# Two neighbouring blocks in one product for half of the off-diagonal products, and the Gram products ahead of `sp` and of half of `up`

## The chip, the cores and the metric

The kernel runs on one core of one Trainium2 chip. The metric is device time in microseconds (us) for one execution. The core has a matrix engine, TensorE (PE in the profile, its weight loads apart as PEld), and VectorE (DVE), ScalarE (ACT), GpSimd (POOL) and the queue of SyncE (SP), which issues transfers.

## What is computed

Three layers in a row. The first is an attention with a state that every token changes; its output is the input of two feed-forward layers.

```python
for t in range(S):                       # S = 768, 4 batches x 8 heads, D = 48
    kt, vt, bt = (k_n[:, :, t], v[:, :, t], beta[:, :, t, None])
    y[:, :, t] = np.einsum('bhd,bhde->bhe', q[:, :, t], state)
    v_old = np.einsum('bhde,bhd->bhe', state, kt)
    state = state + bt[:, :, :, None] * np.einsum('bhd,bhe->bhde', kt, vt - v_old)

a = x @ w_a                              # x: 3072 x 384, w_a, w_b: 384 x 1536
b = x @ w_b
x = a * b @ w_out
h = x @ w_in                             # 384 x 2048
g = np.maximum(h, 0.0) + alpha * np.minimum(h, 0.0)
out = g @ w_out2
```

## The kernel before

**Stages.** The 768 tokens are cut into six stages (`c` = 0 to 5) of 128 tokens, and a stage into two chunks (`j`) of 64. The 32 heads of all batches lie as 16 blocks times two halves of the partitions, called `x` (partitions 0 to 63 and 64 to 127). So a tile such as `ef`, `hw` or `TT` holds 32 blocks (16 for each `j`) of 64 tokens for each half.

**The chain of a stage.** For each stage the attention runs a chain of small products on TensorE, with copies and sums by ACT and DVE between them: `g` (Gram matrices of keys, and of keys with queries), the inversion of a 64 x 64 triangle for every block, `rp` (the part of the values that the state already holds), `up` (the triangle applied to the values), `sp` (the new state) and `yp` (the output). The inversion is done on the two 32 x 32 halves of the diagonal by DVE, and the 32 x 32 corner that is left comes from two products on TensorE, one after the other, both written to banks named `w`: first `w<-hw,ef` (the corner of `ef` times `hw`), whose eight copies go to the other half of `hw`, and then `w<-TT,hw`, whose eight copies go to `TT`. That is `offdiag`, for stages 1 to 5. Stage 0 has a function of its own, `first_sides`, with banks `w` and `xx`.

**How `w` is tiled.** In `offdiag` a product takes one block: 32 partitions deep (the low or the high 32 of a half), a stationary operand of 32 columns and a moving one of 32. There are 32 blocks and two halves, so 64 products for each of the two steps. The order is `i` (0 to 7), `q` (0 to 3), `x`, with block 8q + i at output partitions 32q. The two steps use one half each of the same two banks.

**The Gram products.** `mate` makes the products of a later stage's keys: eight products `g` of 64 x 128, in a bank of their own (`pre`, one buffer), dealt out among the products of another small step, which calls `beside(i)` after its `i`-th round. When the step is done, DVE takes the bank apart (`keep`: one copy to `ef`, two masked products to `Z`). In stages 2 to 4 `rp` and `up` are dealt by a pattern (`uneven`) in which `g` already stands first; `sp` always, and `up` in stage 1, run by the simple loop.

**The feed-forward work.** The first feed-forward layer is made of large products of 128 x 512 (`p`, `o<-g,wu`) that need the attention of a stage, and run beside the chain of the next one. The second layer (`h`, `o<-g,v`) follows from about 614 us on.

**What sets the order.** All instructions are first recorded, then put in order by a planner in the kernel (`Schedule`), which keeps a clock of its own for every engine and, at each step, takes the ready piece of work with the longest chain behind it. Successive small products are one piece (a block); large ones are single. So an edit of one small step may change the order on every engine. All recorded instructions carry line 203, and tiles are named by their names.

Of the kernel before, what the change touches and what calls it, by code (L numbers as in the profile page):

```python
# [5 lines left out]
F32 = mybir.dt.float32  # L6
# [550 lines left out]
class Attention:  # L557
# [80 lines left out]
    def norms(s, L, ef=None, late=False, sq=None):  # L638
# [4 lines left out]
        L["ef"] = ap.tile([128, 32, 64], F32, tag="ef", name="ef", bufs=1) if ef is None else ef  # L643
        sq = L["ef"][:, :, 0:48] if sq is None else sq
# [20 lines left out]
    def scale_values(s, L, j):  # L665
# [7 lines left out]
        s.spend(POOL, 7)  # L673

# [19 lines left out]
    def mate(s, L, j, i4, tag, then=None):  # L694

        def begun():
# [13 lines left out]
            def keep():  # L710
                nc.vector.tensor_scalar(L["ef"][:, j * 16 + i4 : j * 16 + i4 + 4, :], g[:, :, 0, :], -1.0, None, ALU.mult)
# [21 lines left out]
    def keep_keys(s, L, j, i8, g):  # L733

        s.nc.scalar.activation(L["ef"][:, j * 16 + i8 : j * 16 + i8 + 8, :], g, AF.Copy, scale=-1.0)
# [15 lines left out]
    def fold(s, L, j, other=None):  # L751

        e = L["ef"][:, j * 16 : j * 16 + 16, :]
        for sl, copy in ((slice(32, 64), s.nc.scalar.copy), (slice(96, 128), other or s.nc.scalar.copy)):
            copy(e[sl, :, 0:32], e[sl, :, 32:64])
            s.spend(ACT, 2.5)

    def inverting(s, L, room):
# [7 lines left out]
        nc.vector.transpose(a0, L["ef"][:, :, 0:32].rearrange("p a t -> p t a"))  # L766
# [11 lines left out]
    def inverting_halves(s, L, tag):  # L778
# [4 lines left out]
        nc.vector.transpose(eu, L["ef"][:, :, 0:32].rearrange("p a t -> p t a"))  # L783
# [51 lines left out]
    def offdiag(s, L):  # L835
# [4 lines left out]
        room = [s.bank("w").rearrange("p (n i t) -> p n i t", n=2, t=32) for _ in range(2)]  # L840
        for n, (here, left, right, there, to) in enumerate((
            (low, ef[:, :, 32:64], hw, high, hw),
            (high, hw, TT[:, :, 32:64], low, TT[:, :, 32:64]),
        )):
            banks = [t[:, n] for t in room]
            for i in range(8):
                for q in range(4):
                    for x in range(2):
                        nc.tensor.matmul(
                            banks[x][32 * q : 32 * q + 32, i, :],  # L850
                            left[here[x], 8 * q + i, :], right[here[x], 8 * q + i, :], start=True, stop=True,
                        )
            for q in range(4):
                for x in range(2):
                    nc.scalar.copy(to[there[x], 8 * q : 8 * q + 8, :], banks[x][32 * q : 32 * q + 32])
# [3 lines left out]
    def first_sides(s, L):  # L859
# [6 lines left out]
        for j in range(2):  # L866
# [3 lines left out]
            (low, ef[:, :, 32:64], hw, high, hw, [s.bank("w") for _ in range(2)]),  # L870
# [16 lines left out]
    def step(s, c, j, L, mates=(), joined=False, wide=False):  # L887
# [21 lines left out]
        def dealt(parts, beside):  # L909
# [11 lines left out]
            for i in range(8):  # L921
                for n, (o, _) in enumerate(parts):
                    yield n, i, o + i
                beside(i)
# [692 lines left out]
```

## Time and profile before

| | us |
|---|---|
| median of 3 runs | 1011.21 (1011.08 to 1015.61) |
| the profiled execution, own time | 1013.88 |
| its span | 1011.7 |
| PE busy | 991.9 (98%) |
| DVE, POOL, ACT busy | 612.4, 493.9, 461.4 |

A product of f32 leaves two records in the trace, so a block of 64 products is shown as x128. The ends of matrix products are modelled: a record's duration (some 0.19 us for a small one) is how long it takes to come through, and not how much room it takes; the room is read from the starts. A block's last start is its first start plus its length less one record's duration. The chain of work that ended last (part 4 of the page) tells whose time is the kernel's time. The order that the planner makes is shown below as rows of instructions in a row on one engine.

### The profile page before, as it was taken

Reading aid. Unit: us, or ns where it says so; the run is one execution under the profiler, and the core shown is the slowest. Engines: PE = TensorE matmul, PEld = TensorE weight load, DVE = VectorE, ACT = ScalarE, POOL = GpSimd, SP = SyncE. Lnnn points to the kernel's source line nnn. Section 1 sums busy time; section 2 is a strip of 40 time slices with the busy share of each in tenths; the row PEclk is TensorE's granted clock in tenths of the full one; section 3 lists DMA queues with packets and bytes.
Section 4 is the critical chain, followed back from the end, with each engine's and each line's share of the span. In section 5 each row is a group of like instructions: output and inputs, shape, how many; then the busy total and the mean of one; then the engine's idle time right before and its main releaser. Section 6 shows DMA issues by size and latency. Waiting matters only on the chain.

```text
span 1011.7 us, 23674 instructions
## 1 busy us (share of the span) xinstructions
PE 991.9 (98%) x10028; PEld 812.0 (80%) x10028; DVE 612.4 (61%) x1223; ACT 461.4 (46%) x845; POOL 493.9 (49%) x402
## 2 busy tenths in 40 slices
PE   7979999999999999999999999999999999999998
PEld 6767777888888788788878888888888888888886
DVE  7789867856795787567667677343343343433333
ACT  5936784474547355645588785122121221211211
POOL 4467854644664265546557986333333333333332
PEclk8899999999999999999999999999999999999999
DMA  9545423002301210000025542001020020000000
GB/s 216 194 144 181 148 70 94 32 2 66 95 1 33 62 68 1 18 19 31 19 80 174 170 136 84 1 25 38 1 63 1 1 63 0 32 1 1 32 1 32
DMA packets 27082, 61.40 MB, mean 61 GB/s; under 512 B 4320, under 2 KB 8928, under 8 KB 26976
## 3 DMA queue, kind: packets, MB, share of 16 engines
q1 hardware_dynamic: 26544, 59.50, 19.3%
q8 instruction: 78, 1.28, 0.5%
q10 hardware_dynamic: 432, 0.39, 0.1%
q14 instruction: 28, 0.23, 0.1%
HBM read 50.44 MB, written 9.44 MB: 59 GB/s over the span
## 4 chain that ended last, share of the span: by engine, by line
PE 90%; DMA 3%; POOL 2%; issue 2%; ACT 1%; DVE 1%; SPq 0%; DVEq 0%; POOLq 0%; ACTq 0%
PE o L203 33%; PE p L203 26%; PE h L203 19%; PE g L203 3%; PE yp L203 2%; PE spin L203 2%; PE up L203 2%; POOL W L203 1%; PE rp L203 1%; PE sp L203 1%; PE w L203 1%; DMA Z<-in_qt_dram 1%; POOL wu L203 1%; DMA b<-in_beta_dram 1%; DMA Z<-in_w_o_dram 1%
## 5 line engine op out<-in xcount | busy, mean ns | idle before, releaser
L203 PE MATMUL p<-x,wu 128*128 128x512 f32 x1296 | 318.5, 394 | 0.3 <-DVE x L203 0.3
L203 PEld LDWEIGHTS p<-x,wu 128*128 128x128 f32 x1296 | 240.8, 188 | 53.6 <-issue 2.6
L203 POOL TENSOR_TENSOR g<-neg,g 128x512 fp32r<-128x512 f32 x95 | 124.0, 1305 | 261.3 <-ACT g L203 257.8
L203 POOL TENSOR_TENSOR wu<-W,wu 128x384 fp32r<-128x384 f32 (+1 forms) x122 | 173.5, 1425 | 145.1 <-ACT wu L203 143.6
L203 PE MATMUL o<-g,v 128*128 128x512 f32 x870 | 211.5, 388 | 0.0
L203 PE MATMUL h<-x,v 128*128 128x512 f32 x864 | 211.3, 389 | 0.0
L203 DVE TENSOR_SCALAR neg<-h,al 128x512 f32<-128x512 f32 (+1 forms) x97 | 72.2, 744 | 228.8 <-PE h L203 228.7
L203 ACT CAST g<-neg 128x512 fp32r<-128x512 f32 (+1 forms) x97 | 59.8, 616 | 302.9 <-DVE neg L203 288.4
L203 PEld LDWEIGHTS o<-g,v 128*128 128x128 f32 x870 | 162.3, 188 | 33.7 <-ACT g L203 0.2
L203 PEld LDWEIGHTS h<-x,v 128*128 128x128 f32 x864 | 162.2, 188 | 33.7
L203 PE MATMUL o<-g,wu 128*128 128x512 f32 x648 | 164.9, 394 | 1.3 <-ACT g L203 1.1
L203 PEld LDWEIGHTS o<-g,wu 128*128 128x128 f32 x648 | 119.9, 188 | 28.2 <-ACT g L203 1.5
L203 ACT CAST wu<-W 128x768 fp32r<-128x768 f32 (+1 forms) x144 | 96.9, 676 | 80.8 <-PE p L203 59.0
L203 POOL TENSOR_TENSOR g<-a,g 128x512 fp32r<-128x512 f32 x57 | 78.7, 1380 | 40.6 <-ACT g L203 34.6
L203 DVE TENSOR_TENSOR inv<-inv,itmp 128x110 f32<-128x110 f32 (+12 forms) x256 | 75.0, 293 | 8.2
L203 ACT COPY a<-p 128x512 f32<-128x512 f32 x72 | 42.2, 586 | 64.9 <-PE p L203 43.8
L203 DVE SCALAR_TENSOR_TENSOR neg<-h,neg 128x512 f32<-128x512 f32 (+1 forms) x97 | 66.5, 686 | 3.3
L203 PE MATMUL g<-Z 48*64 48x64 f32 (+1 forms) x1024 | 62.8, 265 | 4.5 <-DMA Z<-in_kt_dram 1.9
L203 DVE TENSOR_TENSOR a<-p,a 128x512 f32<-128x512 f32 x59 | 40.5, 687 | 37.9 <-PE p L203 19.7
L203 PEld LDWEIGHTS g<-Z 48*64 48x64 f32 x1024 | 47.3, 148 | 12.4 <-issue 6.1
L203 DVE TENSOR_TENSOR itmp<-inv,gd 128x96 f32<-128x96 f32 (+8 forms) x150 | 40.6, 271 | 9.5 <-ACT gd L203 4.9
L203 ACT CAST g<-a 128x512 fp32r<-128x512 f32 x59 | 36.6, 620 | 6.0 <-DVE a L203 5.5
(110 smaller groups left out, 930.6 us busy)
## 6 DMA issues: line engine op xcount, KB each, us to landing
v<-in_w_o_dram SPq DMA_DIRECT2D x16, 384.0 KB, 3.5
v<-in_w_in_dram SPq DMA_DIRECT2D x16, 384.0 KB, 3.6
Z<-in_kt_dram SPq DMA_DIRECT2D x24, 192.0 KB, 3.6
Z<-in_qt_dram SPq DMA_DIRECT2D x24, 192.0 KB, 4.4
v<-in_vn_dram SPq DMA_DIRECT2D x12, 384.0 KB, 3.2
x2d<-x2s SPq DMA_DIRECT2D x18, 256.0 KB, 2.2
xf<-x2d SPq DMA_DIRECT2D x18, 256.0 KB, 2.7
raw<-in_w_a_dram SPq DMA_DIRECT2D x11, 384.0 KB, 5.6
```

The source lines that it names most:

```text
L203: getattr(s.engines[op.eng], name)(*(real(x) for x in op.a), **{w: real(x) for w, x in op.k.items()})
```

## The change

`offdiag` now takes blocks in neighbouring pairs. Pairs are n = 16m + 2i and the next one (m = 0, 1; i = 0 to 7). Where m + i is even, the pair is one product: a stationary operand of 64 columns (two blocks of 32) and a moving one of 64, still 32 partitions deep, whose result of 64 x 64 holds the two wanted 32 x 32 products on its diagonal, and two that nobody reads. Where m + i is odd, the two blocks stay single products of 32 x 32. A step has 16 products of 64 x 64 and 32 of 32 x 32 instead of 64 of 32 x 32. Since a pair's result takes 64 columns, each step fills both banks whole, and the second writes over the first one's. The copies read the diagonal, in the same number and size (32 x 256).

To make two blocks neighbours without a gap, `ef` is laid out as 2 x 32 x 32 (the half of a block's columns first); its writers and readers (`norms`, `keep`, `keep_keys`, `fold`, the transposes) follow, with the same sizes. In `first_sides` only the name of that half changes; its products stay single.

`beside(i)` is called ahead of a round's products in the simple loops, for `sp` and for `up` where it isn't `uneven`.

```diff
-        L["ef"] = ap.tile([128, 32, 64], F32, tag="ef", name="ef", bufs=1) if ef is None else ef
+        L["ef"] = ap.tile([128, 2, 32, 32], F32, tag="ef", name="ef", bufs=1) if ef is None else ef
...
-                nc.vector.tensor_scalar(L["ef"][:, j * 16 + i4 : j * 16 + i4 + 4, :], g[:, :, 0, :], -1.0, None, ALU.mult)
+                nc.vector.tensor_scalar(s.wide_side(L)[:, j * 16 + i4 : j * 16 + i4 + 4], g[:, :, 0, :].rearrange("p a (h t) -> p a h t", h=2), -1.0, None, ALU.mult)
...
-        room = [s.bank("w").rearrange("p (n i t) -> p n i t", n=2, t=32) for _ in range(2)]
-        for n, (here, left, right, there, to) in enumerate((
-            (low, ef[:, :, 32:64], hw, high, hw),
+        room = [s.bank("w").rearrange("p (i e t) -> p i e t", e=2, t=32) for _ in range(2)]
+        for here, left, right, there, to in (
+            (low, ef[:, 1], hw, high, hw),
             (high, hw, TT[:, :, 32:64], low, TT[:, :, 32:64]),
-        )):
-            banks = [t[:, n] for t in room]
+        ):
             for i in range(8):
-                for q in range(4):
-                    for x in range(2):
-                        nc.tensor.matmul(
-                            banks[x][32 * q : 32 * q + 32, i, :],
-                            left[here[x], 8 * q + i, :], right[here[x], 8 * q + i, :], start=True, stop=True,
-                        )
+                for m in range(2):
+                    for e in ((slice(0, 2),) if (m + i) % 2 == 0 else (slice(0, 1), slice(1, 2))):
+                        at, n = slice(64 * m + 32 * e.start, 64 * m + 32 * e.stop), 16 * m + 2 * i
+                        n = slice(n + e.start, n + e.stop)
+                        for x in range(2):
+                            nc.tensor.matmul(
+                                room[x][at, i, e, :], left[here[x], n, :].rearrange("p a t -> p (a t)"), right[here[x], n, :], start=True, stop=True,
+                            )
             for q in range(4):
+                n = slice(16 * (q // 2) + q % 2, 16 * (q // 2) + 16, 2)
                 for x in range(2):
-                    nc.scalar.copy(to[there[x], 8 * q : 8 * q + 8, :], banks[x][32 * q : 32 * q + 32])
+                    nc.scalar.copy(to[there[x], n, :], room[x][32 * q : 32 * q + 32, :, q % 2, :])
...
             for i in range(8):
+                beside(i)
                 for n, (o, _) in enumerate(group):
...
-                beside(i)
```

What the planner makes of it, in three places. First PE, the block `w<-hw,ef` of stage 2 with what stands around it (`p` and `o` are the large products of 128 x 512), before:

```order
L203 MATMUL p<-x,wu 128x512 x4
L203 MATMUL w<-hw,ef 32x32 x64
L203 MATMUL p<-x,wu 128x512 x14
```

and now:

```order
L203 MATMUL p<-x,wu 128x512 x9
L203 MATMUL w<-hw,ef 64x64 x2
L203 MATMUL w<-hw,ef 32x32 x8
L203 MATMUL w<-hw,ef 64x64 x4
L203 MATMUL w<-hw,ef 32x32 x8
L203 MATMUL w<-hw,ef 64x64 x4
L203 MATMUL w<-hw,ef 32x32 x8
L203 MATMUL w<-hw,ef 64x64 x4
L203 MATMUL w<-hw,ef 32x32 x8
L203 MATMUL w<-hw,ef 64x64 x2
L203 MATMUL p<-x,wu 128x512 x9
```

The block of one kind has become nine runs of two kinds. All ten `w` blocks of stages 1 to 5 read like this.

Second PE, the first block `sp` of stage 2 with its `g`, before:

```order
L203 MATMUL sp<-SU,k 48x48 x2
L203 MATMUL g<-Z 64x128 x2
L203 MATMUL sp<-SU,k 48x48 x4
L203 MATMUL g<-Z 64x128 x2
L203 MATMUL sp<-SU,k 48x48 x4
```

and now:

```order
L203 MATMUL g<-Z 64x128 x2
L203 MATMUL sp<-SU,k 48x48 x4
L203 MATMUL g<-Z 64x128 x2
L203 MATMUL sp<-SU,k 48x48 x4
L203 MATMUL g<-Z 64x128 x2
```

`g` has moved from behind the first round of `sp` to ahead of it, here and in 19 more blocks.

Third ACT in stage 1, from the copies of the first `w` step on (`TT<-w` are the copies of the second; `ef<-k`, `W<-raw` and `wu<-W` belong to the norms of the next stage and to the weights), before:

```order
L203 COPY hw<-w 32x256 x8
L203 COPY TT<-TT 32x32x32 x2
L203 CAST g<-p 128x512
L203 ACTIVATE ef<-k 128x16x48
L203 CAST wu<-W_1597 128x2x384
L203 ACTIVATE W_1739<-raw 128x1152
L203 COPY TT<-w 32x8x32 x8
```

and now:

```order
L203 COPY hw<-w 32x8x32 x8
L203 COPY TT<-TT 32x32x32 x2
L203 COPY TT<-w 32x8x32 x8
L203 CAST g<-p 128x512
L203 ACTIVATE ef<-k 128x768 x2
```

Four instructions that stood ahead of the eight copies now stand behind them. On PE, 16 large products stand between the two `w` blocks of stage 1 (20 before) and 8 between the second one and `rp` (19 before); from the first `w` block of stage 1 to its last `yp` there are 114 large products either way. Over the whole program PE has 145 runs of large and of small work in turn, before and now.

## Rows read from the trace of the kernel before

**Rows 1.** The page: busy time of the engines, and the chain that ended last.
```profile
PE 991.9 (98%) x10028; PEld 812.0 (80%) x10028; DVE 612.4 (61%) x1223; ACT 461.4 (46%) x845; POOL 493.9 (49%) x402
...
PE 90%; DMA 3%; POOL 2%; issue 2%; ACT 1%; DVE 1%; SPq 0%; DVEq 0%; POOLq 0%; ACTq 0%
```

**Rows 2.** Busy time by stretch: length, then PE, PEld, DVE, ACT, POOL, PEclk.
```profile
72.70:76.00 3.30, 3.03 (x31) 2.52 (x26) 2.83 (x8) 2.04 (x5) 2.02 (x3) 0.50 1.04 408
...
355.00:450.00 95.00, 95.00 (x1382) 77.27 (x1374) 66.61 (x164) 51.73 (x98) 49.64 (x40) 1.00 0.08 24
...
540.00:1011.00 471.00, 467.01 (x2066) 386.32 (x2064) 214.67 (x291) 140.63 (x256) 193.44 (x149) 1.00 0.14 43
```

**Rows 3.** Timeline of PE, stage 4: start, length, instruction, count.
```profile
402.61 1.29 PE L203 MATMUL w<-hw,ef 32*32 32x32 f32 x128
403.83 3.01 PE L203 MATMUL p<-x,wu 128*128 128x512 f32 x12
406.68 1.52 PE L203 MATMUL o<-g,wu 128*128 128x512 f32 x6
408.13 1.29 PE L203 MATMUL w<-TT,hw 32*32 32x32 f32 x128
```

**Rows 4.** Instructions by tile: records, ns of one (least/median/most), first and last start.
```profile
L203 PE MATMUL w<-hw,ef x768: 184/191/213, 47.4 to 504.4; 32*32 32x32 f32 x192
...
L203 PE MATMUL up<-v,TT x768: 204/218/254, 53.1 to 533.5; 64*64 64x48 f32 x192
...
L203 PE MATMUL sp<-SU,k x704: 205/205/278, 56.8 to 521.1; 64*48 64x48 f32 x176
...
L203 PE MATMUL yp<-Z,SU x1536: 216/219/244, 58.4 to 538.3; 112*32 112x64 f32 x96, 128*32 128x64 f32 x96
```

**Rows 5.** Timeline of PE, stage 5: `up`, `sp` and `yp` among large products.
```profile
516.84 1.15 PE L203 MATMUL up<-v,TT 64*64 64x48 f32 x64
...
520.41 0.94 PE L203 MATMUL sp<-SU,k 64*48 64x48 f32 x64
...
524.45 2.00 PE L203 MATMUL yp<-Z,SU 112*32 112x64 f32 x128
526.38 1.66 PE L203 MATMUL o<-g,wu 128*128 128x512 f32 x6
```

**Rows 6.** Timeline of PE, stage 0: three kinds of small products one behind the other.
```profile
57.23 1.28 PE L203 MATMUL sp<-SU,k 64*48 64x48 f32 x46
58.44 2.00 PE L203 MATMUL yp<-Z,SU 112*32 112x64 f32 x128
60.38 0.72 PE L203 MATMUL rp<-SU,Z 48*64 48x48 f32 x14
```

**Rows 7.** Timeline of ACT, stage 4: the copies out of `w`.
```profile
403.93 3.01 ACT L203 COPY hw<-w 32x256 f32<-32x256 f32 x8 [2.00 <-PE w L203]
```

**Rows 8.** Timeline of PE, stage 2: first and second `sp` with `g`.
```profile
236.02 0.25 PE L203 MATMUL sp<-SU,k 64*48 64x48 f32 x2
236.03 0.33 PE L203 MATMUL g<-Z 48*64 48x128 f32 x2
...
238.90 0.33 PE L203 MATMUL g<-Z 48*64 48x128 f32 x2
```

**Rows 9.** Timeline of DVE, stage 2: `Z<-g,mask`, with which it leaves the bank of `g`.
```profile
237.51 0.85 DVE L203 TENSOR_TENSOR Z<-g,mask 64x256 f32<-64x256 f32 x2
```

**Rows 10.** Timeline of PE, stage 1: the second `w` block and `rp`.
```profile
127.35 1.19 PE L203 MATMUL w<-TT,hw 32*32 32x32 f32 x117
129.24 0.28 PE L203 MATMUL w<-TT,hw 32*32 32x32 f32 x11 [0.69 <-issue]
...
134.81 1.52 PE L203 MATMUL rp<-SU,Z 48*64 48x48 f32 x64 [0.74 <-ACT TT L203]
```

**Rows 11.** Timeline of ACT, stage 1: the copies around the second `w` block.
```profile
126.81 2.11 ACT L203 COPY TT<-TT 32x1024 f32<-32x1024 f32 x2
...
132.17 2.98 ACT L203 COPY TT<-w 32x256 f32<-32x256 f32 x8
```

More of the change, by code (lines that the diff above doesn't have):

```diff
@@ L642, in norms @@
         b2 = L["b"].rearrange("p j a -> p (j a)")
-        L["ef"] = ap.tile([128, 32, 64], F32, tag="ef", name="ef", bufs=1) if ef is None else ef
-        sq = L["ef"][:, :, 0:48] if sq is None else sq
+        L["ef"] = ap.tile([128, 2, 32, 32], F32, tag="ef", name="ef", bufs=1) if ef is None else ef
+        sq = L["ef"].rearrange("p h a t -> p (h a t)")[:, : 32 * 48].rearrange("p (a d) -> p a d", d=48) if sq is None else sq
         ss = ap.tile([128, 32], F32, tag="ss", name="ss", bufs=2)
@@ L673, in scale_values, with wide_side @@
         s.spend(POOL, 7)
+    def wide_side(s, L):
+        return L["ef"].rearrange("p h a t -> p a h t")
     def gram_keys(s, L, j, i8, tag):
@@ L733, in keep_keys @@
     def keep_keys(s, L, j, i8, g):
-        s.nc.scalar.activation(L["ef"][:, j * 16 + i8 : j * 16 + i8 + 8, :], g, AF.Copy, scale=-1.0)
+        s.nc.scalar.activation(s.wide_side(L)[:, j * 16 + i8 : j * 16 + i8 + 8], g.rearrange("p a (h t) -> p a h t", h=2), AF.Copy, scale=-1.0)
     def mask_queries(s, L, j, i8):
@@ L751, in fold @@
     def fold(s, L, j, other=None):
-        e = L["ef"][:, j * 16 : j * 16 + 16, :]
+        e = L["ef"][:, :, j * 16 : j * 16 + 16]
         for sl, copy in ((slice(32, 64), s.nc.scalar.copy), (slice(96, 128), other or s.nc.scalar.copy)):
-            copy(e[sl, :, 0:32], e[sl, :, 32:64])
+            copy(e[sl, 0], e[sl, 1])
             s.spend(ACT, 2.5)
@@ L765, in inverting @@
         nc.scalar.copy(room.rearrange("p t s -> p (t s)")[:, 0:1024:33], L["bt"])
-        nc.vector.transpose(a0, L["ef"][:, :, 0:32].rearrange("p a t -> p t a"))
+        nc.vector.transpose(a0, L["ef"][:, 0].rearrange("p a t -> p t a"))
         nc.vector.tensor_tensor(a0[:, :, 0:8], a0[:, :, 0:8], bt[:, :, 0:8], ALU.mult)
@@ L782, in inverting_halves @@
         bt = s.turned(L)
-        nc.vector.transpose(eu, L["ef"][:, :, 0:32].rearrange("p a t -> p t a"))
+        nc.vector.transpose(eu, L["ef"][:, 0].rearrange("p a t -> p t a"))
         nc.gpsimd.tensor_tensor(eu, eu, bt, ALU.mult)
@@ L869, in first_sides @@
         stages = (
-            (low, ef[:, :, 32:64], hw, high, hw, [s.bank("w") for _ in range(2)]),
+            (low, ef[:, 1], hw, high, hw, [s.bank("w") for _ in range(2)]),
             (high, hw, TT[:, :, 32:64], low, TT[:, :, 32:64], [s.bank("xx", "ab") for _ in range(2)]),
@@ L967, in step @@
             for i in range(8):
+                beside(i)
                 for n, (o, _) in enumerate(group):
@@ L971, in step @@
                         nc.tensor.matmul(sps[n][at : at + 48, i, :], bk[sl, j, o + i, :], SU[x][sl, o + i, 0:48], start=True, stop=True)
-                beside(i)
             for n, (_, hs) in enumerate(group):
@@ L1258, in attn_moe_kernel @@
         squares = lambda: xp.tile([128, 32, 48], F32, tag="x0", name="sq")
-        finish(A.norms(L, wp.tile([128, 32, 64], F32, tag="w8", name="ef0"), sq=squares()))
+        finish(A.norms(L, wp.tile([128, 2, 32, 32], F32, tag="w8", name="ef0"), sq=squares()))
         N = A.load(1)
```

## The prediction

> **What bounds the kernel now.** I read the page's busy shares first, then the chain that ended last. PE is busy for 98% of the span, and 90% of the chain is PE [rows 1]; every other engine has a third or more of its time free. Then busy time by stretch: in stage 4, from 355 to 450 us, PE is busy all of the 95.00 us at a clock of 1.00, while ACT works 51.73 and DVE 66.61 [rows 2]. So from stage 2 on, what an edit does to the time that PE gives to its small blocks is what it does to the kernel. Only in stage 1 does PE still wait here and there [rows 10].
>
> Next, how much room things take on PE. Large products: 2066 in 467.01 us of busy time [rows 2], 0.226 us each. A `w` block: from one to the next in stage 4 are 5.52 us (402.61 to 408.13) with 18 large products between [rows 3], 18 x 0.226 = 4.07, so a block costs 1.45. Within the block the 128 records start at a steady pace: length 1.29 less one record's 0.191 [rows 3, 4] over 127 steps is 8.65 ns, 1.11 us for all. The other 0.34 us is paid at the two ends, 0.17 at each change between large and small.
>
> **The change, part by part.**
>
> *The products of `w`.* A step had 128 records of 32 stationary columns. It will have 32 of 64 columns (16 pairs) and 64 of 32. What does a record of 64 columns cost? In the same way from stage 5: `sp` with 48 columns (0.94 less 0.205, over 63) has a pace of 11.7 ns, `up` with 64 (1.15 less 0.218, over 63) 14.8 [rows 4, 5]. From 32 to 48 to 64 columns the pace goes 8.65, 11.7, 14.8: it goes by the columns of the weights and hardly by the number of products. I take `up`'s 14.8, since it too has 64 columns and works in both halves of the partitions in turn, though 64 deep where a pair is 32: 32 x 14.8 + 64 x 8.65 = 1.03 us instead of 1.11, a saving of 0.08 per block. Bounds: 0.28 if a record costs 8.65 whatever its width (32 records fewer), and 0 if a pair costs as much as its two blocks.
>
> *What stands between the products.* The block had one shape and has nine runs of two shapes in turn, so eight changes of shape inside. Does a change cost anything? The trace has four kinds, all of them from one division of the matrix engine to another. Large to `w` and back: 0.17 each (above). Large to `up` or `sp` and back: `up` starts 3.57 us ahead of `sp`, 10 large products between take 2.26, 64 x 14.8 ns are 0.95, so 0.36 stays for two, 0.18 each; `sp` to `yp` with 13 between gives the same 0.18 [rows 5]. Small to small, in stage 0: the last `sp` starts at 57.23 + 1.28 - 0.205 = 58.305, the first `yp` at 58.44, 0.135 later where the pace is 0.012; the last `yp` starts at 60.22, the first `rp` at 60.38, 0.16 later where the pace is 0.014 [rows 4, 6]. So 0.12 and 0.15 more. The one that is most telling is `yp` to large: both work on all partitions, only the columns differ (32 and 128), and the large product still starts 0.15 us behind the last `yp` (526.23 to 526.38) [rows 4, 5]. By contrast `sp` and `g`, with 48 and 64 columns and 64 and 48 partitions, stand in one block and follow each other within 0.01 us [rows 8]. So a gap isn't paid for a mere difference of sizes. Whether a pair and a single, alike in depth (32 partitions) and unlike in width (64 columns and 32), share a division or change it, no row shows. Bounds: 0, as between `sp` and `g`, and 0.18. I take a change of division, since both sides fill what they stand on (32 and 64 whole columns), where `sp`'s 48 leave 16 of 64 empty; the price is the middle of 0.12 to 0.18, 0.15. Eight of them: 1.20 per block.
>
> The Trainium skill, "TensorEngine Tiling (Array Packing)", section Tiling Modes, has 32 x 64 and 32 x 32 as two modes, and says that changing the mode, and not just the tile, drains TensorE. The trace agrees for the four kinds above, with 0.12 to 0.18 us each; for these two modes no row here shows it. With the rule a block is 1.12 us longer, without it 0.08 shorter.
>
> Sum for a block: 1.20 - 0.08 = +1.12; ten blocks (two in each of stages 1 to 5), all on PE's path: **+11.2 us**. Its ends: 8 x 0.12 - 0.28 = 0.68 and 8 x 0.18 - 0 = 1.44, so 6.8 to 14.4.
>
> *The copies and banks.* The eight ACT copies have the same size, 3.01 us in all [rows 7], and begin when the block is over. That the second step now overwrites the first one's banks adds no wait: it needs `hw`, which those very copies write. In stage 4, 15 or 16 large products (3.4 us) stand between the two blocks in the new order, about as long as the copies with their hand-over; if that is short, PE waits some tenths per stage. The new layout of `ef` keeps all sizes on ACT and DVE, which have room [rows 2]: nothing.
>
> *`g` ahead.* In 20 blocks (16 of `sp`, 4 of `up`) `g` starts the block. Now it starts 0.01 us behind `sp` (236.02, 236.03) [rows 8]; its products are the longer stream of the block, so the block may end that much sooner, by 0.2 to 0.4 us in all. What it could cost: `g` now stands at the head of the queue, so if its bank isn't free, `sp` behind it waits, and DVE for `sp`. DVE leaves the bank at 237.51 + 0.85 = 238.36 and the next `g` starts at 238.90 [rows 8, 9]: 0.54 us of room. I take -0.3, bounds -1 and 0.
>
> *The new order.* The runs of large and small work are as many as before, 145, so no ends are won or lost there. From stage 2 on the order differs by a few large products. In stage 1 it differs more: the second step's copies start behind `TT<-TT` (which ends at 128.92) instead of behind four other instructions (132.17) [rows 11], 3.2 us sooner, but `rp`, which waits for them, stands behind 8 large products and not 19, 2.5 us sooner. Before, PE stood 0.69 us inside the second `w` block with no releaser named ("issue"), and 0.74 for ACT ahead of `rp` [rows 10]. I leave this at 0, bounds -1.4 (both gone) and +1.4 (both twice).
>
> Sum: 11.2 - 0.3 + 0 = +10.9. The profiled execution took 1013.88 with a span of 1011.7, so it would take 1024.8; the median of the runs is 2.67 lower, and 1011.21 + 10.9 = **1022.1 us**. This case's own range is 1018 to 1025: the ends of the sum, 4.4 and 15.8 above, hold only if all go one way.
>
> **The rivals.** *No gap between a pair and a single* (chance 0.29, the other side): both belong to one division, as `sp` and `g` do. For it speaks that both are 32 partitions deep, and that in rows 6 depth and width change together. Then ten blocks save 0.08 each, `g` 0.3: -1.1, 1010.1 us, with stage 1 between 1008.7 and 1011.5. The point from which it decides is 0.01 us for a change: below that the kernel isn't slower.
>
> *The count of products rules* (0.03): 32 records fewer at 8.65 ns, 0.28 per block, no gap: 1008.1. Against it stand the paces of 11.7 and 14.8. The Trainium skill, same page, section Performance Considerations, gives each matmul some 60 cycles of overhead whatever its size; as an estimate at 2.4 GHz 25 ns, so 32 fewer would save 0.8 us per block, and the kernel would take some 1003. The trace disagrees: its records follow each other every 8.65 ns.
>
> *A smaller gap* (0.07): a change waits, but only about half of what rows 6 show, 0.06: 8 x 0.06 - 0.08 = 0.4 per block, 1014.9 (1012.5 to 1018).
>
> *The clock falls too* (0.04): with eight gaps a block leaves PE idle enough that a stretch runs at 0.50, 1.2 GHz, as between 72.7 and 76.0, behind a long wait [rows 2]. Half of such a 3.3 us stretch is lost, 1.65; once in each of five stages is 8 us on top, 1030.
>
> **How the numbers follow.** The forecast has 0.57. The range leaves out the clock (0.04), the count (0.03), some of the no-gap case below 1009.5 (0.05) and of the forecast above 1025 (0.04): 1009.5 to 1025. A measurement here can tell 0.5% (5 us) from no change. Slower by more than that, over 1016.3: nearly all of the forecast (0.56), the clock, and some of the smaller gap: 0.63. Within it: no gap, the count, most of the smaller gap: 0.35. Faster: 0.02, since even both waits of stage 1 and the count's saving come to 1.4 + 2.8 + 1.0.
>
> **What would show it.** Timeline of PE, stage 4: from one `w` block to the next, less 0.226 for each large product between, should be 2.6 us (1.45 before). Within a block the starts should show eight steps of 0.12 us or more between records of 32 and of 64 columns; if they are 0.015 or less, the first rival holds. In `sp` blocks `g` should be first, with the block's end where it was within 0.03. PE's waits in stage 1 should sum to 0 to 2.8. Granted clock: 1.00 from 76 us on. The forecast is wrong if the block is 1.4 us or shorter, or if a wait for ACT appears between the two `w` blocks that takes more than the gaps.

## The result: 1.46% slower

The changed kernel takes 1027.57 us (median of 5 runs, 1023.79 to 1029.21), beside 1011.67 for the kernel before on the same chip: 1.0146 times [1.0126, 1.0167], 15.9 us more. The forecast was 10.9 us more (1022.1, with a range to 1025.0). The direction and the main mechanism hold: the ten `w` blocks cost 10.0 us. The other 6 come from two places that the forecast set at nothing: some 4, by an estimate, from more time at the low clock (a granted clock of 0.50, that is 1.2 GHz), the rest from the new order of stage 1.

The profiled execution took 1029.21 us, with a span of 1027.5 (before 1011.7). Its page, the engines and the chain, as in [rows 1]:

```profile
PE 1006.9 (98%) x9708; PEld 820.8 (80%) x9708; DVE 622.0 (61%) x1230; ACT 460.0 (45%) x842; POOL 489.2 (48%) x398
...
PE 89%; POOL 4%; ACT 2%; issue 2%; DMA 2%; DVE 1%; DVEq 0%; POOLq 0%; SPq 0%
```

PE has 320 records fewer (10 steps with 16 products fewer, two records each) and is busy 15 us longer: the lost time is inside PE's busy time, so a list of waits doesn't show it. The stretches that answer to [rows 2], with one in stage 1 (length, then PE, PEld, DVE, ACT, POOL, PEclk, DMA share, GB/s):

```profile
126.30:129.70 3.40, 3.40 (x9) 2.62 (x10) 1.42 (x2) 3.25 (x10) 2.94 (x2) 0.51 0.20 58
355.00:450.00 95.00, 95.00 (x1284) 76.66 (x1283) 66.57 (x161) 50.91 (x97) 46.13 (x38) 1.00 0.10 31
```

In stage 4 PE is again busy for all of the 95 us at full clock, with 98 records fewer: 64 of them are records that the pairs of its two blocks save, the rest is work that no longer falls into the stretch. PE's timeline of stage 4, as in [rows 3]:

```profile
414.72 2.29 PE L203 MATMUL w<-hw,ef 32*64 32x64 f32 x96
416.94 2.35 PE L203 MATMUL p<-x,wu 128*128 128x512 f32 x9
419.13 1.75 PE L203 MATMUL o<-g,wu 128*128 128x512 f32 x7
420.81 2.29 PE L203 MATMUL w<-TT,hw 32*64 32x64 f32 x96
```

The block is 2.29 long, where it was 1.29. From one `w` to the next are 6.09 us with 16 large products between; less 16 x 0.226 that leaves 2.47, as against 1.45 before. (2.6 was forecast.) The starts of the block's 96 records, one by one, show where the time goes (the first half; the second repeats it, and a step of 100 ns stands within the first and the last two pairs):

```
 record   starts at   next one after (ns)
   3      414.833     146     last of a pair      -> first single (4)
  19      415.079     120     last single         -> first of a pair (20)
  23      415.219      87     pair at output partitions 64 to 127 -> pair at 0 to 63
  27      415.326     147     last of a pair      -> first single
  43      415.572     121     last single         -> first of a pair
  all others: 6 or 7
```

So each change of shape stops the starts for 0.12 us (to pairs) or 0.147 (to singles), the sizes that [rows 6] showed between other kinds. A further step of 0.09 follows a few records behind each change to pairs; in exchange, records in between follow at 6.6 ns and not at 8.65. What counts is the sum. I take it for a block with both its ends: from the last large start ahead of it to the first one behind it, less 0.227. Before it is 1.309 us in stages 2 to 5, now 2.311, eight times each: +1.00.

`g` is first in the `sp` blocks (as in [rows 8]; 245.29 for `g`, 245.30 for `sp`), and these blocks take 1.112 and 1.120 us instead of 1.126 and 1.134 in stages 2 to 5.

Where the 15.8 us of the span are. The residual of a stage is its time from `w` to `w`, less 0.2267 for each large product in it:

| | before | after | difference |
|---|---|---|---|
| start to the first `p` | 73.9 | 76.6 | +2.6 |
| stage 1, residual | 22.27 | 27.10 | +4.8 |
| stages 2, 3 and 4, residual each | 20.03 | 22.02 | +2.0 each, +6.0 |
| from the first `w` of stage 5 to the last large product, residual | 12.70 | 15.05 | +2.4 |
| the rest | | | 0.0 |

Stages 2 to 4 are two blocks of +1.00 each and nothing else, three times over, to the hundredth. The start is chance: PE runs the same 1422 records there in both, and over all the kernels below, which share them, the first `p` comes at 68.5 to 78.3 us. What differs is the clock (columns as above):

```profile
0.00:76.50 76.50, 65.60 (x1422) 54.15 (x1422) 59.87 (x130) 44.95 (x79) 38.97 (x53) 0.86 0.59 164
```

It is 0.86 here; before, 0.90 over the first 73.90 us.

The clock bears on the medians, too. Of the changed kernel's five executions the one with a mean granted clock of 0.993 took 1023.79 us; the other four, at 0.986 to 0.990, took 1027.03 to 1029.21. Beside the experiments stand 79 executions of the kernel before; the 20 of them with 0.993 have a median of 1012.28. So at the same mean clock the change costs 11.5 us. As an estimate from these numbers, some 4 of the 15.9 are time at the low clock. Why the changed kernel's executions had more of it isn't shown.

That leaves stage 1, which lost 2.8 us beyond its two blocks. PE there, as in [rows 10]:

```profile
123.92 2.29 PE L203 MATMUL w<-hw,ef 32*64 32x64 f32 x96 [0.19 <-DVE hw L203]
126.14 0.65 PE L203 MATMUL o<-g,wu 128*128 128x512 f32 x1
126.58 3.70 PE L203 MATMUL p<-x,wu 128*128 128x512 f32 x9
...
136.64 1.52 PE L203 MATMUL rp<-SU,Z 48*64 48x48 f32 x64 [0.71 <-ACT TT L203]
...
139.90 1.66 PE L203 MATMUL p<-x,wu 128*128 128x512 f32 x6
143.12 0.33 PE L203 MATMUL g<-Z 48*64 48x128 f32 x2 [1.57 <-DVE Z L203]
```

Two things are new. Nine `p` right behind the first `w` block take 3.70 us (2.35 in stage 4), in the stretch with the clock at 0.51, that is 1.2 GHz for nearly all of it: some 1.6 us lost with the `o` ahead of them. And the second block of `g` and `up` waits 1.57 us for DVE; with its ends it takes 2.82, before 1.17. The two `sp` blocks behind it take 1.48 and 1.33 instead of 1.13 (+0.55). The 0.69 us of "issue" in the second `w` block [rows 10] is gone, so that this block grew by 0.13 only; the 0.74 ahead of `rp` has stayed. Without the low clock, stage 1 lost 1.2 us more than two blocks of +1.00. So of the 15.8 us of this execution 10.0 are the blocks, 4.2 go with low clock (2.6 at the start, 1.6 in stage 1), and 1.6 are left for the new order. ACT's copies, as in [rows 11], show that the new order does what was read from it, and no more:

```profile
129.45 2.12 ACT L203 COPY TT<-TT 32x1024 f32<-32x1024 f32 x2
133.97 3.01 ACT L203 COPY TT<-w 32x256 f32<-32x256 f32 x8 [2.40 <-PE w L203]
```

The copies now stand directly behind `TT<-TT`, but wait 2.40 us for the block that fills their bank. What DVE does meanwhile is what the forecast didn't read. Before, and after:

```profile
136.40 1.70 DVE L203 TENSOR_TENSOR v<-rp,v 128x384 f32<-128x384 f32 x3
138.13 0.69 DVE L203 TENSOR_TENSOR g<-p,g 128x512 fp32r<-128x512 f32 x1
138.74 0.41 DVE L203 TENSOR_SCALAR ef<-g 128x256 f32<-128x256 f32 x1
139.07 0.85 DVE L203 TENSOR_TENSOR Z<-g,mask 64x256 f32<-64x256 f32 x2
```

```profile
138.23 0.55 DVE L203 TENSOR_TENSOR v<-rp,v 128x384 f32<-128x384 f32 x1
138.69 1.80 DVE L203 TENSOR_REDUCE ss<-ef 128x16 f32<-128x768 f32 x2
140.53 1.12 DVE L203 TENSOR_TENSOR v<-rp,v 64x384 f32<-64x384 f32 x2
141.68 0.42 DVE L203 TENSOR_SCALAR ef<-g 128x256 f32<-128x256 f32 x1
142.12 0.86 DVE L203 TENSOR_TENSOR Z<-g,mask 64x256 f32<-64x256 f32 x2
```

`ss<-ef`, the sums of squares in `norms`, now stands between two `v<-rp`: 1.80 us ahead of `Z<-g,mask`, for which PE waits.

### The profile page after: what moved, and what is told of

It is laid out like the page before. It is cut to its first block, busy times and chain, and to the rows that moved or that the text cites. A ratio compares the mean times of both kernels' runs of the same rounds, so it can differ in the third digit from the quotient of the medians.

```text
span 1027.5 us, 23032 instructions
## 1 busy us (share of the span) xinstructions
PE 1006.9 (98%) x9708; PEld 820.8 (80%) x9708; DVE 622.0 (61%) x1230; ACT 460.0 (45%) x842; POOL 489.2 (48%) x398
## 4 chain that ended last, share of the span: by engine, by line
PE 89%; POOL 4%; ACT 2%; issue 2%; DMA 2%; DVE 1%; DVEq 0%; POOLq 0%; SPq 0%
PE o L203 32%; PE p L203 25%; PE h L203 19%; PE g L203 3%; PE w L203 2%; PE yp L203 2%; PE spin L203 2%; DMA Z<-in_qt_dram 2%; PE up L203 2%; POOL W L203 1%; POOL wu L203 1%; PE sp L203 1%; PE rp L203 1%; POOL g L203 0%; POOL f L203 0%
## 5 line engine op out<-in xcount | busy, mean ns | idle before, releaser
L203 POOL TENSOR_TENSOR g<-a,g 128x512 fp32r<-128x512 f32 x53 | 71.8, 1355 | 41.1 <-ACT g L203 38.1
L203 POOL TENSOR_TENSOR f<-f,v 128x384 int32<-128x384 int32 x32 | 36.4, 1149 | 8.3 <-DVE v L203 8.3
```

The source lines that it names most:

```text
L203: getattr(s.engines[op.eng], name)(*(real(x) for x in op.a), **{w: real(x) for w, x in op.k.items()})
```

## The experiments

**What a pair, a single and a change cost.** The theory: a change of shape stops PE for a fixed time; all else in the block is small. First the changed kernel with single products only, so that the layout and `g` ahead are left of the change:

```diff
-                    for e in ((slice(0, 2),) if (m + i) % 2 == 0 else (slice(0, 1), slice(1, 2))):
+                    for e in (slice(0, 1), slice(1, 2)):
```

> The changed kernel with single products only (64 of 32 x 32 per step, new layout of ef and whole banks kept, g ahead kept). Theory (the gap at each change between pair and single products is what costs): a w block with its ends falls from 2.31 us to 1.31 as before, eight blocks of stages 2 to 5 win 8 us, and the kernel is at 1011 to 1016, with what is left due to stage 1 and the start. Rival (the whole banks and the new layout slow the products or their copies, or g ahead does): the w blocks stay near 2.3, or the kernel stays above 1020 with short blocks. On the start (first large product of the feed-forward work at 73.9 us before, 76.6 after): if it is chance of an execution, the four kernels of this call spread over 73 to 77; if the layout of ef causes it, all four lie near 76.5.

Measured: 1013.51 us, 1.0008 [0.999, 1.0026]; a block 1.308. So without pairs there is no loss that shows, whatever the layout and `g` do, though stage 1 has a residual of 23.4 us: its order differs from that of the kernel before, too.

All pairs (`for e in (slice(0, 2),):`):

> The changed kernel with all 32 pairs of a step as products of 64 x 64, none single: no change inside a block. Theory (pace by the columns of the weights, 14.8 ns for 64): 64 x 14.8 = 0.95 us and the ends 0.24, so 1.19 us per block, 0.12 less than before; kernel at 1009 to 1014. Rival (a pair product itself is dear): 64 records at 46 ns, 3.0 us and more per block; kernel above 1030. Rival (a pair of 32 x 64 costs as much as two blocks, 17.3): 1.35.

Measured: 1015.87 us, 1.0024 [1.0006, 1.0042]. The blocks are shorter than before, 1.181:

```profile
407.94 1.16 PE L203 MATMUL w<-hw,ef 32*64 32x64 f32 x64
409.03 2.33 PE L203 MATMUL p<-x,wu 128*128 128x512 f32 x9
```

and yet the kernel is not faster: stage 1 has a residual of 25.2 us (22.3 before), with 1.58 us of wait at `rp` and 1.57 at the second `g` and `up`. With 1.308 for singles and 1.181 for pairs, a block of half and half without changes would take 1.245. The changed kernel's 2.311 is 1.07 more: 0.133 for each of eight changes.

The same 16 pairs and 32 singles, sorted, so that one change is left:

```diff
+            for wide in (True, False):
                 for i in range(8):
                     for m in range(2):
-                        for e in ((slice(0, 2),) if (m + i) % 2 == 0 else (slice(0, 1), slice(1, 2))):
+                        if ((m + i) % 2 == 0) != wide:
+                            continue
+                        for e in (slice(0, 2),) if wide else (slice(0, 1), slice(1, 2)):
```

> The changed kernel with the same 16 pairs and 32 singles per step, but all pairs first and then all singles: one change inside a block instead of eight. Theory (0.135 us for each change): a w block with its ends takes 2.31 - 7 x 0.135 = 1.37 us; kernel at 1012 to 1017. Rival (a pair product itself is dear, 1.0 us for 32 records more than the pace of its columns): 2.3 us as in the changed kernel, kernel at 1024 to 1029.

Measured: 1017.96 us, 1.0047 [1.0028, 1.0065]; a block 1.398:

```profile
408.15 1.38 PE L203 MATMUL w<-hw,ef 32*64 32x64 f32 x96
409.46 2.35 PE L203 MATMUL p<-x,wu 128*128 128x512 f32 x9
```

0.153 for the one change, and seven changes fewer give back 0.91 us of a block. This is the same work in another sequence inside the block (around it every engine runs in the changed kernel's order), so nothing but the changes can have cost that. Again the kernel is slower than its blocks: ten times 0.09 is 0.9 us, measured are 5.0.

More changes, 15 and 31, with the same products (15: two pairs, then four singles; 31: pairs and singles of the two halves one by one):

```diff
+                for e, x in ((pair, 0), (pair, 1), (one, 0), (one, 1), (two, 0), (two, 1)):
...
+                for e, x in ((pair, 0), (one, 0), (pair, 1), (one, 1), (two, 0), (two, 1)):
```

> The same 16 pairs and 32 singles per step, in runs of 2 pairs and 4 singles: 15 changes of shape instead of 8 within a block. Theory (each change costs the same 0.133 us as with eight): a block takes 1.245 + 15 x 0.133 = 3.24 us between large products, 0.93 more than the changed kernel's 2.31, and stages 2 to 4 take 23.9 us each less large products; kernel 1.022 to 1.026 times the one before. Rival (the price of a change rises with their number, as the run with 31 changes suggests at 0.21 or more): 4.4 us or more a block, and stretches at half clock; 1.035 or more.

> The changed kernel with the same 16 pairs and 32 singles per step, dealt so that a block changes 31 times between the two instead of 8. Theory (each change costs about the same, 0.133 us over a base of 1.245 from the blocks of one kind): 1.245 + 31 x 0.133 = 5.4 us for a w block with its ends, kernel about 30 us above the changed one, 1055 to 1062. Rival (a change costs less when the runs are short, since little is under way): below 4 us.

Measured with 15: 1045.77 us, 1.0323 [1.0278, 1.0367]; a block 3.718, 0.165 for a change. That lies between the two expectations (3.24 and 4.4). With 31: 1103.8 us, 1.0903 [1.0878, 1.0928], beyond what was expected; a block takes 7.7 to 9.5 us. The price isn't all: the clock comes on top. First 15 changes, then 31, from stage 2 on (windows as above, and PE's timeline):

```profile
224.80:228.20 3.40, 3.40 (x18) 2.66 (x17) 0.00 (x0) 2.92 (x9) 0.00 (x0) 0.50 0.00 0
...
323.80:327.20 3.40, 3.40 (x10) 2.64 (x9) 0.00 (x0) 3.28 (x10) 0.00 (x0) 0.50 0.02 5
```

```profile
225.03 3.79 PE L203 MATMUL p<-x,wu 128*128 128x512 f32 x9
228.66 1.55 PE L203 MATMUL o<-g,wu 128*128 128x512 f32 x6
230.14 3.70 PE L203 MATMUL w<-TT,hw 32*64 32x64 f32 x96
```

```profile
237.60:247.80 10.20, 10.20 (x70) 7.58 (x69) 0.00 (x0) 3.85 (x10) 0.00 (x0) 0.50 0.00 0
```

```profile
243.72 4.21 PE L203 MATMUL p<-x,wu 128*128 128x512 f32 x9
...
249.24 7.71 PE L203 MATMUL w<-TT,hw 32*64 32x64 f32 x96
```

With 15 changes one 3.4 us stretch at 0.50 follows a block in each of stages 1 to 5, and nine large products take 3.79 us where the changed kernel's in stage 4 took 2.35. With 31 the clock falls inside the blocks, for 6.8 to 10.2 us at a time. With eight changes it fell once, from stage 1 on, in the changed kernel: behind the first block of stage 1.

**`g` behind again**, pairs and singles in turn (the two `beside(i)` moved back):

> The changed kernel with g behind the first round again, as before; pairs and singles in turn kept. Theory: w blocks stay at 2.31 us, sp blocks go back from 1.11 to 1.13, and the wait of g for DVE in stage 1 (1.9 us in two places in the changed kernel) is smaller or moves to sp; the kernel is at 1020 to 1027. Rival 1 (g at the head of the queue causes the wait of stage 1): the wait goes, 2 us less than the changed kernel. Rival 2 (the new order of stage 1 causes it): the wait stays at over 1 us with g behind.

Measured: 1025.93 us, 1.0135 [1.0107, 1.0163]; the `sp` blocks are back at 1.125 and 1.133 us, the second block of `g` and `up` still takes 2.58, and every engine but for the place of `g` runs in the changed kernel's order. So `g` ahead gains 16 x 0.013 = 0.2 us and isn't what waits in stage 1.

**Where the loss is.** In turn in stages 2 to 5 alone, then in stage 1 alone, and all pairs in stages 2 to 5 (each time singles elsewhere):

```diff
+                    for e in ((slice(0, 2),) if c > 1 and (m + i) % 2 == 0 else (slice(0, 1), slice(1, 2))):
...
+                    for e in ((slice(0, 2),) if c == 1 and (m + i) % 2 == 0 else (slice(0, 1), slice(1, 2))):
...
+                    for e in ((slice(0, 2),) if c > 1 else (slice(0, 1), slice(1, 2))):
```

> The changed kernel with single products in stage 1, pairs and singles in turn in stages 2 to 5 as there. Theory: eight blocks with eight changes each, 8 x 1.0 = 8.0 us above before, and no wait of g for DVE above 1 us in stage 1: kernel 7 to 9 us slower than before, 5 to 7 faster than the changed kernel. Rival (the rest above the ten blocks' 10 us is not stage 1's order): 11 us or more slower than before.

> The changed kernel with pairs and singles in turn in stage 1 alone, singles in stages 2 to 5. Theory: two blocks with eight changes, 2.0 us less the 0.9 of a fetch wait that stood in one of them, and stage 1's order with the two sums of ss between the subtractions of v, 2 to 4 us: 4 to 6 us slower than before. Rival (the order of stage 1 is not what costs): 1 to 2 us slower.

> The changed kernel with all products of w as pairs in stages 2 to 5, and all as single ones in stage 1. Theory (changes inside a block cost, a block of pairs alone is 0.127 us shorter, and what else was lost was stage 1's new order): eight blocks at 1.18 win 1.0 us, sp blocks 0.2, stage 1 as in the kernel with singles; 0.5 to 2 us faster than before. Rival (the loss of 2 to 4 us beside the blocks, seen with all pairs, comes from stages 2 to 5): slower than before by 2 us or more.

Measured: 1021.54 us (1.0080 [1.0061, 1.0098], 8.8 us more) for stages 2 to 5, whose eight blocks account for 8.0; 1019.68 (1.0064 [1.0043, 1.0084], 6.9 us more) for stage 1 alone, whose two blocks account for 2.0; and 1012.97 (1.0004 [0.9991, 1.0017]) for the late pairs, where a gain of 1 us or so had been expected and none shows. So stages 2 to 5 pay for the changes and hardly anything else. With stage 1 changed, some 5 us (2.4 to 6.5 by the interval) are paid for something else; the profile of that kernel shows 25.5 in stage 1, 3.2 above the kernel before, blocks included, so not all of it stands there.

**What stage 1 pays for: the scratch, first.** `norms` keeps the squares in the space of `ef`. In the new layout the second half's squares lie over blocks of the first half, so `ef<-g` has to wait for both sums, which would explain why both stand together on DVE. Three kernels have the scratch laid so that each half stays with its own blocks:

```diff
+                to = L["ef"][:, :, part].rearrange("p h a t -> p h (a t)")[:, :, 0:384].rearrange("p h (b d) -> p h b d", d=48)
```

> The changed kernel, with one difference: the scratch in which the squares of the keys are kept (inside ef) is laid so that the squares of each half of the blocks stay within that half's own blocks, as in the kernel before. In the changed kernel the second half's squares lie over blocks of the first half, so the first write to ef waits for both sums of squares. Theory (the new layout's scratch is what lengthens stage 1: both sums stand together on DVE ahead of the writes to ef and Z): stage 1 less its large products falls from 25.5 us (the runs in turn without the stretch at half clock) to 23 to 24.5, the second block of g and up falls from 2.8 to about 1.2, and the kernel takes 1.0 to 2.5 us less than the changed one, 1.010 to 1.0135 times the kernel before. Rival (what counts is where the planner puts the sums between the subtractions, or the blocks' shorter plan, not whose blocks the scratch lies over): stage 1 stays at 25 to 26, the block at 2.5 to 2.8, ratio 1.0135 to 1.015. Stages 2 to 4 stay at 22.0 each by both.

> All 64 products of a step as 32 pairs of 64 x 64, no single left, g ahead, and the scratch of the squares laid as in the kernel before. If the scratch is what lengthened stage 1 in the run with all pairs (25.2 us there against 22.3 and 23.4 with single products), stage 1 comes to 22.0 to 23.5, and the pairs' saving of 0.13 us in each of ten blocks is left over: 0.5 to 1.5 us faster than the kernel before, ratio 0.9985 to 0.9995. If it isn't, the time is that of all pairs, ratio 1.002 to 1.003.

> Single products only, g ahead, the new layout of ef but with the scratch as before: what is left of the change is the layout's strides and g's place. Theory (neither costs anything): 1.000 times the kernel before within 0.0015, stage 1 less its large products 22.3 to 23.5. Rival (the layout's strides or g ahead cost some of stage 1's time): ratio 1.001 or more, stage 1 at 23.5 to 25.

Measured: in turn, 1028.35 us, 1.0146 [1.0115, 1.0176], as slow as without, though the interval reaches into what the theory had; stage 1's residual is 27.9, in an execution with a stretch of 10.2 us at low clock there. On DVE one sum of 0.94 us stands between the subtractions, where two took 1.80, and PE no longer waits for `Z`; instead it waits 1.62 us for ACT at `rp` (0.71 in the changed kernel). `rp` takes 4.06, the first `g` and `up` block 2.23 and the second 1.77, but all three lie in the low stretch, so their lengths can't be compared with others. All pairs: 1014.41, 1.0016 [0.9995, 1.0037], stage 1 at 25.8, with a wait of 2.2 us for ACT at `rp` and 6.8 us at low clock, here without any change of shape:

```profile
125.30:132.10 6.80, 5.95 (x116) 4.91 (x117) 4.05 (x6) 6.65 (x11) 1.83 (x1) 0.50 0.22 58
```

Only with singles does the scratch work as thought: 1013.44, 1.0005 [0.9987, 1.0022], and stage 1 has a residual of 22.3, that of the kernel before. So the scratch does bear on whether both sums stand together, but no gain in time shows: with pairs, mending it exchanges one wait for another. How much of stage 1 it would have saved at full clock isn't shown.

**The order.** A block of pairs, or of pairs and singles, is planned at 0.870 us and with fewer instructions, one of singles at 0.928. That is enough for the planner to make another order. So the order is held fixed, and the products are exchanged. `e18_singles_after_order` has singles in exactly the changed kernel's order on each engine; the two others have the new products in the order of the singles with the mended scratch. The traces bear this out, and show one thing more: that last order, below called the good one, is that of the kernel before. On DVE, ACT and POOL every instruction, and on PE every block and large product, stands in its sequence.

```diff
+                t.planned = 64 if t.cost > 0.8 and name == "w" else k
+                t.cost = 0.0145 * 64 if t.planned > k else t.cost
...
-                late = fetched(b, cost, 2 if t.large else 4 * len(t.ops))
+                late = fetched(b, cost, 2 if t.large else 4 * t.planned)
```

> Single products of 32 x 32 only, but with the changed kernel's own layout and its own order on every engine (the planner is told that a w block costs what it took the changed one to cost). Theory (order): the second block of g and up still takes 2.8 us and stage 1 less its large products 23.5 to 25 us (25.5 to 27.1 less 2.0), against 22.3 before, ratio 1.001 to 1.003. Rival (products): stage 1 at 22.3 to 22.6, that block at 1.2, ratio 0.9995 to 1.0005.

> Pairs and singles in turn as in the changed kernel, scratch of the squares as before, and the planner is told that a w block costs what 64 single products cost, so that every engine runs in the order of the kernel with single products and that scratch (which measured 1.0005). Only the products inside the ten w blocks differ from it. Theory (the extra of stage 1 is the planner's order): stage 1 less its large products is 22.3 + 2 x 1.0 = 24.3 us, stages 2 to 4 22.0 each, and the kernel takes ten times 1.0 more than before: 1.0095 to 1.0105. Rival (the products themselves make stage 1 slow): stage 1 at 25.5 or more, ratio 1.0115 to 1.0145.

> As e15_same_order, but all products of a w block are pairs, 32 of 64 x 64. Theory (order): stage 1 at 22.3 - 0.25 = 22.05 us, stages 2 to 4 at 19.7, the kernel 1.3 us (ten blocks) and 0.2 (g ahead) faster than before: ratio 0.9980 to 0.9990. Rival (products): stage 1 at 25, ratio 1.001 to 1.003 as in the two earlier runs with all pairs.

Measured: singles in the changed kernel's order, 1017.20 us, 1.0051 [1.0038, 1.0064], 5.2 us more, without a single pair. DVE and PE in stage 1 (timelines):

```profile
132.88 1.80 DVE L203 TENSOR_REDUCE ss<-ef 128x16 f32<-128x768 f32 x2
...
136.31 0.86 DVE L203 TENSOR_TENSOR Z<-g,mask 64x256 f32<-64x256 f32 x2
```

```profile
134.92 0.31 PE L203 MATMUL up<-v,TT 64*64 64x48 f32 x2 [0.77 <-issue]
135.16 1.65 PE L203 MATMUL p<-x,wu 128*128 128x512 f32 x6
137.31 0.33 PE L203 MATMUL g<-Z 48*64 48x128 f32 x2 [0.50 <-DVE Z L203]
```

The sums stand in the same place, and PE waits for `Z` again, 0.50 us; another 0.77 in the first block has no releaser named. The two blocks of `g` and `up` take 4.05 us together, where the singles in their own order with the mended scratch have 2.35; the residual is 25.4 against 22.3. That was expected at 2.8 us in the second block alone and at a ratio of 1.001 to 1.003: right that the order alone costs, too small in size, and wrong on where: the second block takes 1.74.

In turn, in the good order: 1022.09, 1.0100 [1.0087, 1.0113], 10.1 us more, the number that the theory had: ten changed blocks at 1.00 each. Stage 1 has no wait but one, at its start:

```profile
120.28 2.29 PE L203 MATMUL w<-hw,ef 32*64 32x64 f32 x96 [0.20 <-DVE hw L203]
122.50 3.91 PE L203 MATMUL p<-x,wu 128*128 128x512 f32 x9
126.25 1.55 PE L203 MATMUL o<-g,wu 128*128 128x512 f32 x6
...
122.60:126.00 3.40, 3.40 (x8) 2.67 (x9) 1.04 (x2) 3.26 (x10) 3.10 (x3) 0.50 0.21 58
```

and in this order, too, the clock falls behind the first block (3.91 us for nine `p`; the last row is the stretch), as in the changed kernel; with `g` behind, and with changes in stage 1 alone, it didn't in the one execution profiled. That eight changes bring it down at times is likely, but not shown. The residual of 23.7 is below the 24.3 expected, and that it comes so near is in part luck: the two blocks cost 1.12 and not 2.0, since the 0.69 us of "issue" is gone, `rp` with its ends takes 1.17 instead of 2.36, and the low clock takes some 1.5 back.

All pairs in the good order: 1011.82, 0.9999 [0.9982, 1.0015]. Blocks of 1.181 and a residual of 19.71 in each of stages 2 to 4 (before 20.03) are there, and stage 1 is at 22.31; but the 1.5 us that were expected can't be told from nothing with runs that spread over 9 us. No version here beats the kernel before by what can be measured.

10.1 for the products in the good order, and 5.2 for the order without the products: 15.3, of the 15.9 us measured. With the singles and mended scratch in the order of before (`e14_singles_scratch`), four kernels make a table of times, as ratios to the kernel before:

| | singles | in turn |
|---|---|---|
| order of before, mended scratch | 1.0005 | 1.0100 |
| changed order | 1.0051 | 1.0146 |

In either order the products cost 9.6 us, and with either products the order, the scratch included, 4.7; each ratio is uncertain by 0.0013 to 0.0020. The profiles put the cost of the order in stage 1 lower: 25.4 - 22.3 = 3.1 with singles (neither has low clock there), 27.1 - 23.7 = 3.4 in turn (both have one such stretch).

## Why the prediction was right and wrong

*What bounds the kernel.* Right. PE is busy 98% in both, and in stages 2 to 4 the residual grows by just what the two blocks grow.

*The pace of a pair.* 14.8 ns for a record, taken from `up`; with all pairs the 63 steps of a block take 0.94 us, about 15. The saving of half a block of pairs was put at 0.08, and is 0.064 (half of 1.308 - 1.181). Right.

*The changes.* That a pair of 32 x 64 and a single of 32 x 32 change the division of the matrix engine, as `sp` and `yp` do, was open. That each change costs is now shown by the sorted block: seven changes fewer, 0.91 us less. The reason that the forecast gave for its choice, that both fill what they stand on, was not tried. The Trainium skill, "TensorEngine Tiling (Array Packing)", section Tiling Modes, says that a change of mode drains TensorE; for these two modes the trace now agrees, with steps of 0.12 and 0.147 us. The price was put at 0.15 for each and is 0.133 in sum. With it the block's +1.12 became +1.00, and ten blocks +10.0 instead of +11.2: inside the bounds. The rivals "no gap", "the count of products" and "a smaller gap" are out.

*`g` ahead.* Forecast -0.3, bounds -1 and 0; measured -0.2. Its bank was late nowhere in stages 2 to 4.

*The copies and banks.* Right in stages 2 to 4: no wait between the two steps.

*The new order.* This step failed. It was put at 0, bounds -1.4 and +1.4, from ACT's copies and from the two waits of PE that the trace of before had. With the products held the same, the order costs 3.1 to 3.4 us in stage 1 by the profiles and 4.7 in all by the medians. Against the kernel before, the changed one shows only 1.2 of it in stage 1 (without the clock), since its second `w` block gained 0.9: that this still lies within the bound is luck, for none of it is what the bound was made of. What went wrong is which engine was read. The forecast compared PE and ACT around the second `w` block, and "DVE has room" was taken from its share of 70% in stage 4. In stage 1 DVE is what `Z`, and so the next `g` and `up`, wait for, and there the order had moved `ss<-ef` into the middle of the subtractions: 1.80 us in front of the write that PE needs. In the changed kernel that is the wait of 1.57 and the 0.30 at the first `sp`; with singles in that order it is 0.8, and the rest lies in the `w` and `yp` blocks and in waits with no releaser named. The place of the sums could be read from the order of DVE before any run. Bounding a reordered stage by the waits that the old order happened to have was the wrong bound, since a new order makes waits of its own. The new layout was put at nothing, and with singles that holds (1.0008, and 1.0005 with the mended scratch); its scratch is part of what the order costs.

*The clock.* This step failed as well, and it is the larger: the sum had no term for it, and the clock was to be 1.00 from 76 us on. The rival had one stretch at 1.2 GHz in each of five stages, 8 us, at a chance of 0.04. One came in the profiled execution, behind the first block of stage 1, and cost the 1.6 us that the rival gave for one. With 15 changes it came in all five. With the start of the program, the low clock is some 4 us of the median, by the estimate above; at a mean clock of 0.993 the change costs 11.5. That this is so near the 10.9 of the forecast is luck: blocks that cost 1.2 less than was forecast and an order that cost some 1.6 more make it up.

*The range.* It left out all above 1025.0 with 0.04, since the upper ends of the terms should not meet. The products came out below the forecast, and the median still lies above the range, by the clock, which had no bound, and the order together. The fastest execution, 1023.79, lies inside it.

What stays open: one profile of the singles in the changed order shows 3.1 us of its 5.2 in stage 1 and 0.3 in stage 5. The rest is likely clock, and so is a like part of the 10.1 of the products in turn: in the 79 executions of the kernel before, 1 us more at the low clock (twice the missing share of the mean clock, times the span) goes with 0.32 us more of time (0.24 to 0.41 in the four sets beside the experiments), and the medians of that low-clock time are 20.3 us for these singles, 20.4 for the products in turn and 14.1 for the kernel before beside them: as an estimate, some 2 us in each. Which of the two, the planned length or the number of instructions, moves the order was not taken apart. And why the price of a change rises from 0.133 with eight to 0.165 with 15 isn't settled: with shorter runs there are fewer of the quick 6.6 ns steps behind a change to give some of it back, but that was only read, not tried. Nor is it shown what brings the clock down in kernels with eight changes or none.

## What to carry to other kernels

Count the changes of tile shape in a stream of small products before counting products: here one change costs as much as 15 small records, so sort by shape, or keep to one shape. Where a planner sets the order, an edit to one block's planned length is an edit to every engine: read the new order of each engine that somebody waits for, and bound the reordered stage by what may now stand ahead of those waits, not by the waits of the old order. To take product and order apart, hold the order fixed and exchange the products, and then the other way round; the two parts should add up to the whole. And compare executions of like mean clock before a difference of a few us is given to a cause.

## What the runs showed of the hardware

A change between products of 32 x 64 and of 32 x 32 stops the starts for 0.147 us (to singles) or 0.121 (to pairs), net 0.13 to 0.17 each, though both are 32 partitions deep and PE is "busy" all through. A product that computes four 32 x 32 tiles to use two costs no more than the two alone (1.181 us a block against 1.308). And the granted clock fell to 0.50 behind or within blocks with many changes, while the profile counted PE as busy for all of that time: in five stages with 15 changes a block, and for 6.8 to 10.2 us at a time with 31. With eight changes it fell once, for 3.4 to 10.2 us, or not at all, from stage 1 on; with none it fell once, for 6.8 us, in a kernel whose PE was in a wait of 2.2 us for ACT as the stretch began.
